# Another table of steps and engines for a three-layer kernel (attention, routed attention, convolution-gated FFN) on one core

## The chip, the core and the metric

The kernel runs on one NeuronCore of a Trainium2 chip. The metric is the device time of one execution in microseconds. Five engines work side by side, each through its own list of instructions in order: TensorE (PE, matmuls and transposes into PSUM banks), VectorE (DVE), ScalarE (ACT), GpSimd (POOL) and SyncE (SP), which here only issues DMAs. An engine stops at an instruction until the semaphores it waits for are there, and everything behind it on that engine stops too.

## The reference

Three layers follow each other, in float32. First, causal attention of 4 batches, 12 heads, 448 positions, 64 values a head. Second, a layer of four experts, each a small attention with its own weights, of which two are chosen for a position by a gate. Third, a feed-forward layer with a convolution of three taps over the positions and a sigmoid gate.

```python
attn_out = softmax(mask(q @ k.T / 8)) @ v                    # 4 x 12 heads, 448 x 448, causal
x = concat_heads(attn_out)                                   # 4 x 448 x 768
logits = x @ w_gate; w = softmax over the 2 largest of 4 experts
out = sum_e [e chosen] * w_e * softmax(mask(q_e @ k_e.T / 8)) @ v_e @ wo_e    # q_e, k_e, v_e = x @ wq/wk/wv[e]
h = relu(out @ w_in)                                         # 768 -> 1024
conv = conv_w[0]*h[s-1] + conv_w[1]*h[s] + conv_w[2]*h[s+1]
result = (h * sigmoid(conv)) @ w_out                         # 1024 -> 768
```

## The kernel before

Heads are worked in pairs: job A(b, p) is pair p (6 of them) of batch b in the first layer, job M(b, p) a pair of experts (2) in the second. The 448 positions are four blocks of 112. In a head, PE makes the scores of a block of rows (L632, L675), DVE their negative maximum over the causal part and a copy into SBUF (`rowmax`, L688, into P_A or P_M), ACT the exponential with its sum (`soft`, L697), DVE the reciprocal of the sums (L705, L708), one of three engines the scaling by it (`norm`, through `copy`, L349 on ACT, L351 on POOL, L355 on DVE), PE the transposes of the probabilities (L728), ACT or DVE their evacuation into PT (`evac`), and PE the product with v (L799).

For precision most operands of matmuls are split in two: hi, a rounded copy, and lo, the operand minus hi; a product is then three matmuls. So around the attention there is much work from SBUF to SBUF: `hi` is a `copy` (L349, L351, L355) and `lo` a subtraction (`two`, L358, on POOL or DVE). This is done for q and k of the later batches (nat into sk_A), for the weights of the experts (praw into wqk and wvg), for w_in (wraw over wm into whl, then folded with wo on PE at L920, three pieces of 12 matmuls a quarter), and for w_out (woraw over wom into wohl, with sums and differences of blocks, `combine`, for a multiplication scheme of 7 in place of 8 block products). The wohl tiles go to DRAM and come back as ws for the last stage, where PE multiplies them (L1473) with operands that are again split from SBUF tiles (ux, up, us, uq, uv).

All this is laid down as 3108 steps with what each needs and frees. A step's engine can be one of several:

```python
def of_two(n):
    return {"POOL": pool_tt(n), "DVE": dve(n)}
def of_one(n):
    return {"POOL": pool_ts(n), "DVE": 60 + 0.54 * n, "ACT": act_sb(n)}
```

Nothing is decided there when the kernel is built: a packed table, `ORDER`, lists all steps in one sequence, each with the engine it runs on, and `Program.run` (called at L1582) emits them in that order. So the table alone sets what stands before what in the list of each engine, which engine does a step, which PSUM bank a step gets, and when SP issues a DMA. `run` keeps a rough account of times only to put short runs of filler matmuls (L1580) where PE is likely to stand idle.

Of the kernel before, what the change touches and what calls it, by code (L numbers as in the profile page):

```python
# [1644 lines left out]
```

## Time and profile before

| | us |
|---|---|
| runs of the kernel | 489.45, 487.45, 489.25; median 489.25 |
| the profiled execution | 490.9 |
| its span, first to last instruction | 489.1 |

| engine | busy us | share of the span | instructions |
|---|---|---|---|
| PE | 476.2 | 97% | 3126 |
| DVE | 394.3 | 81% | 1145 |
| ACT | 342.9 | 70% | 956 |
| POOL | 346.4 | 71% | 491 |

The profile is of one execution. Busy time of PE includes time in which a matmul waits in its pipeline, so that the timeline's idle times before a matmul are what tells of a wait. In a timeline row a bracket at the end says how long the engine was idle before the first instruction of the row, and which instruction ended that. The mean granted clock of PE over the span is 0.991 of 2.4 GHz.

### The profile page before, as it was taken

The numbers are of one execution on the slowest core, as the hardware profiler recorded it, in microseconds if no ns is written. First come the engines' busy times: TensorE is split into PE (matmuls) and PEld (weight loads), VectorE is DVE, ScalarE is ACT, GpSimd is POOL, SyncE is SP. The second block draws the span as 40 slices with busy tenths as digits, with TensorE's granted clock in tenths as the row PEclk, the third lists the DMA queues.
The fourth block names the chain that finished last, engine by engine and source line by source line (L and its number), as shares of the span: only waits on it lengthen the run. The fifth ranks groups of instructions, "written<-read, shape, count | busy, mean of one in ns | idle before, by whom it ended". The sixth has DMA issues, their size and how long they took to land.

```text
span 489.1 us, 9977 instructions
## 1 busy us (share of the span) xinstructions
PE 476.2 (97%) x3126; PEld 401.3 (82%) x3126; DVE 394.3 (81%) x1145; ACT 342.9 (70%) x956; POOL 346.4 (71%) x491
## 2 busy tenths in 40 slices
PE   8999999999899999999999989999999999999996
PEld 7667787889679788878988867888789999999986
DVE  4899996999999888998789986277879987886372
ACT  3999987999888778998888976168985654432100
POOL 3969987879888768898888874015686486794820
PEclk9899999999999999999999989999999999999999
DMA  6854657988866964796874638364756676752022
GB/s 188 254 168 131 174 157 190 255 269 227 251 202 188 272 195 123 206 256 193 255 189 139 154 111 278 124 231 161 238 199 209 254 257 215 238 192 94 20 76 95
DMA packets 45413, 93.26 MB, mean 191 GB/s; under 512 B 4784, under 2 KB 26800, under 8 KB 45360
## 3 DMA queue, kind: packets, MB, share of 16 engines
q1 hardware_dynamic: 45360, 92.63, 63.3%
q8 instruction: 25, 0.41, 0.4%
q14 instruction: 28, 0.23, 0.2%
HBM read 60.72 MB, written 25.69 MB: 177 GB/s over the span
## 4 chain that ended last, share of the span: by engine, by line
PE 81%; ACT 6%; DVE 5%; POOL 3%; DMA 2%; issue 2%; POOLq 0%; DVEq 0%; ACTq 0%
PE bank L1473 21%; PE bank L799 11%; PE bank L993 11%; PE bank L728 10%; PE bank L675 9%; PE bank L1340 8%; PE bank L1044 6%; ACT P_A L697 3%; PE bank L632 3%; DMA woraw<-in_w_out_dram 2%; PE bank L920 2%; DVE P_A L688 2%; PE bank L1580 2%; POOL P_A L351 1%; ACT P_A L349 1%
## 5 line engine op out<-in xcount | busy, mean ns | idle before, releaser
L697 ACT ACTIVATE P_A<-P_A,nm_A 112x448 f32<-112x448 f32 (+3 forms) x192 | 99.6, 521 | 17.1 <-DVE nm_A L688 14.9
L688 DVE CUSTOM_DVE_ANT_0 P_A<-bank,mask 112x448 f32<-112x448 f32 (+3 forms) x192 | 78.6, 440 | 14.6 <-PE bank L632 7.9
L358 POOL TENSOR_TENSOR sk_A<-nat,sk_A 128x448 fp32r<-128x448 f32 (+1 forms) x70 | 81.2, 1160 | 8.2 <-ACT sk_A L349 2.6
L993 PE MATMUL bank<-xT,wqk 128*128 128x448 f32 x288 | 66.4, 372 | 0.0
L728 PE MATMUL bank<-ident,P_A 112*112 112x112 f32 x480 | 60.8, 265 | 2.5 <-ACT PT_A L349 1.4
L351 POOL TENSOR_SCALAR P_A<-P_A,r_A 112x224 f32<-112x224 f32 (+3 forms) x99 | 48.9, 507 | 12.2 <-PE bank L675 3.5
L728 PEld LDWEIGHTS bank<-ident,P_A 112*112 112x112 f32 x480 | 49.2, 135 | 9.6 <-ACT PT_A L349 2.4
L993 PEld LDWEIGHTS bank<-xT,wqk 128*128 128x128 f32 x288 | 51.8, 188 | 4.4 <-DVE lg L1064 0.5
L675 PE MATMUL bank<-sk_A 128*112 128x112 f32 (+3 forms) x288 | 51.8, 307 | 1.4 <-DVE nm_A L688 1.2
L799 PE MATMUL bank<-PT_A,v 112*64 112x448 f32 (+3 forms) x384 | 49.9, 405 | 0.2 <-DVE xT L831 0.2
L1473 PE MATMUL bank<-up,ws 128*128 128x448 f32 x198 | 48.5, 366 | 0.0
L1361 DVE SCALAR_TENSOR_TENSOR bank<-h,cw,bank 128x448 f32<-128x448 f32 x64 | 43.4, 686 | 5.2 <-ACT bank L1359 4.2
L799 PEld LDWEIGHTS bank<-PT_A,v 112*64 112x64 f32 x384 | 25.4, 136 | 23.5 <-issue 12.3
L675 PEld LDWEIGHTS bank<-sk_A 128*112 128x112 f32 x288 | 39.7, 175 | 5.9 <-DVE nm_A L688 1.5
L1044 PE MATMUL bank<-wvg,xT 128*112 128x260 f32 x288 | 44.2, 292 | 0.1
L349 ACT ACTIVATE P_A<-P_A,r_A 112x448 f32<-112x448 f32 (+3 forms) x83 | 41.4, 527 | 3.9 <-DVE r_A L708 3.8
L349 ACT ACTIVATE PT_A<-bank 112x336 f32<-112x336 f32 (+1 forms) x92 | 41.3, 469 | 2.9 <-PE bank L728 2.5
L351 POOL TENSOR_SCALAR P_M<-P_M,r_M,g_w 112x112 f32<-112x112 f32 (+3 forms) x61 | 35.6, 595 | 9.7 <-DVE r_M L708 5.5
L1473 PE MATMUL bank<-us,ws 128*128 128x448 f32 x171 | 41.4, 367 | 0.0
L1473 PEld LDWEIGHTS bank<-up,ws 128*128 128x128 f32 x198 | 37.2, 188 | 3.3
L1044 PEld LDWEIGHTS bank<-wvg,xT 128*112 128x112 f32 x288 | 36.8, 177 | 1.9 <-issue 1.5
L697 ACT ACTIVATION_READ_ACCUMULATOR P_A<-P_A,nm_A 112x1 f32 x192 | 36.8, 192 | 0.0
(184 smaller groups left out, 1069.1 us busy)
## 6 DMA issues: line engine op xcount, KB each, us to landing
nat<-in_qk_dram SPq DMA_DIRECT2D x72, 224.0 KB, 4.1
ws<-wset SPq DMA_DIRECT2D x7, 1536.0 KB, 7.7
wset<-wohl SPq DMA_DIRECT2D x18, 512.0 KB, 4.1
g<-g SPq DMA_DIRECT2D x32, 224.0 KB, 2.5
wraw<-in_w_in_dram SPq DMA_DIRECT2D x12, 512.0 KB, 5.2
woraw<-in_w_out_dram SPq DMA_DIRECT2D x12, 512.0 KB, 5.6
v<-in_v_dram SPq DMA_DIRECT2D x24, 224.0 KB, 5.0
out_dram<-osb_c SPq DMA_DIRECT2D x24, 224.0 KB, 2.0
```

What stands on the lines that cost most here:

```text
L349: nc.scalar.activation(dst, src, AF.Copy, scale=scale)
L351: nc.gpsimd.tensor_scalar(dst, src, scale, 1.0 if scale2 is None else scale2, ALU.mult, ALU.mult)
L358: (nc.gpsimd if e == "POOL" else nc.vector).tensor_tensor(dst, a, b, op)
L675: nc.tensor.matmul(sp[:CP], t[:, j.o[h], m * CP : (m + 1) * CP], t[:, j.o[h] + k, :w], start=(k == 2), stop=(k == 1),)
L688: nc.vector.tensor_tensor_reduce(rows(i), st["s", i][:CP, :w], mask[:, S - w :], -SCALE, 3.0e38, ALU.add, ALU.min, st["nm"][:, i : i + 1],)
L697: nc.scalar.activation(rows(i), rows(i), AF.Exp, bias=st["nm"][:, i : i + 1], scale=-1.0, accum_out=st["sm"][:, i, 0:1],)
L728: nc.tensor.transpose(pt[:CP, o : o + CP], rows(i)[:, kt * CP : (kt + 1) * CP], ident[:CP, :CP])
L799: nc.tensor.matmul(st["ov"][h * D : (h + 1) * D, kt * CP : S], j.v[:, kt, h, :], j.PT[h][:, col_base[kt] : col_base[kt] + S - kt * CP], st ...
L993: nc.tensor.matmul(st["ps"][:, :S], proj["wqk"][:, a, cc, w, p * P : (p + 1) * P], xT[b, cc][:, b2, :], start=(cc == 0 and (a, b2) == PASS ...
L1044: nc.tensor.matmul(st[i][:CP, :VW], xT[b, cc][:, a, i * CP : (i + 1) * CP], proj["wvg"][:, b2, cc, :], start=(cc == 0 and (a, b2) == PASSE ...
L1361: nc.vector.scalar_tensor_tensor(y, h, w, y, ALU.mult, ALU.add)
L1473: nc.tensor.matmul(ps(pb)[:, :S], wset[s][:, a, m, c2 * P : (c2 + 1) * P], unit(operands[q, c2, name][0])[:, b2], start=(c2 == 0 and (a, b ...
```

## The change

Only the table `ORDER` is another: the same 3108 steps, in another sequence, with another engine for 345 of them. It comes from a search over sequences and engines in which a DVE step from SBUF to SBUF that coincides with work on POOL was charged extra time; that charge isn't in the kernel's code. Its rows tell a reader nothing, so one of each side is shown.

```diff
--- before.py
+++ after.py
@@ -27,74 +27,74 @@
 
 ENGINES = ("ACT", "DVE", "PE", "POOL", "SP", "")
 ORDER = (
-    "c-jrt$4}b{gD_xMa0UNdz!hA<6<om;cW?z)+_6n&B_LS|NLB(ep9Ew+2}o7~@~%Y5N|dY=U=Bd$03?S%a-hrs$R0461CSgjIZ)n}D6`V{J%7c6"
...
+    "c-jrt$4}b{gD_xM+;In2a0OS~!4+J=75sAncMO@8fMg{gSqaE|5|H^MAXy2McO^<zqGY8&=0KSPkQ{*I0Avn8_JGM8C^-bk0m!=&kXh;bp1<P3"
...
 )
```

Counted in the built programs, PE has the same matmuls in both (2785 as listed, the same 23 filler instructions in runs of 10, 11 and 2), and SP the same 293 instructions. The counts that differ most:

| step | on DVE | on POOL | on ACT |
|---|---|---|---|
| two-input steps of the last stage (L358, ux, up, us, uq, uv) | 28 to 42 | 52 to 38 | |
| the same, both inputs in one tile | 9 to 5 | 7 to 11 | |
| hi of wohl, 512 columns | 10 to 13 | | 8 to 5 |
| hi of wohl, 256 columns | 2 to 4 | | 4 to 2 |
| lo of whl | 3 to 0 | 9 to 12 | |
| subtraction of halves of wom | 3 to 1 | 9 to 11 | |
| normalisation of P_A, 336 columns | 7 to 0 | 25 to 23 | 16 to 25 |
| hi of sk_A from nat | 1 to 1 | 21 to 18 | 14 to 17 |

All SBUF-to-SBUF steps of L353, L355 and L358 on DVE together are 5 more.

The first place is the hi step of wohl_1_4 of the last conversion of w_out (numbers 4017 before and 4087 now): the third score row maximum of a head follows it on DVE. DVE before (the rows that only fetch a maximum are left out in the lists of DVE):

```order
L688 ISA P_A_5_1_3997,nm_A_5_1_3998<-bank_62,mask 112x448
...
L355 TENSOR_SCALAR wohl_1_4_4017<-wom_1_1_3830 128x512
L688 ISA P_A_5_1_3997,nm_A_5_1_3998<-bank_65,mask 112x336
...
L688 ISA P_A_5_1_3997,nm_A_5_1_3998<-bank_61,mask 112x112
...
L355 TENSOR_SCALAR PT_A_3_1_1_4022<-bank_63 112x336
```

DVE now:

```order
L688 ISA P_A_5_1_3970,nm_A_5_1_3971<-bank_62,mask 112x336
...
L688 ISA P_M_1_1_4010,nm_M_1_1_4011<-bank_61,mask 112x336
...
L355 TENSOR_SCALAR wohl_1_4_4087<-wom_1_1_3887 128x512
L705 TENSOR_REDUCE r_A_5_1_3972<-sm_88 112x4
L355 TENSOR_SCALAR PT_A_3_1_0_4018<-bank_63 112x336
L708 RECIPROCAL r_A_5_1_3972<-r_A_5_1_3972 112x4
L688 ISA P_A_5_0_4105,nm_A_5_0_4106<-bank_61,mask 112x224
```

The hi step stands behind two row maxima as it did, but behind it comes the sum and reciprocal of P_A_5_1's rows (L705, L708), and the evacuation of PT; the next row maxima are those of another head.

POOL at the same place, before:

```order
L351 TENSOR_SCALAR P_A_3_1_3796<-P_A_3_1_3796,r_A_3_1_3798 112x112
L358 TENSOR_TENSOR wom_1_1_3830<-wom_1_0_3829,wom_1_1_3830 128x256
L351 TENSOR_SCALAR P_A_3_0_3868<-P_A_3_0_3868,r_A_3_0_3870 112x448
L358 TENSOR_TENSOR wohl_1_0_3993<-wom_1_0_3829,wohl_1_0_3993 128x512
L358 TENSOR_TENSOR sk_A_5_3885<-nat_5_0_3886,sk_A_5_3885 128x448
L358 TENSOR_TENSOR sk_A_5_3885<-nat_5_0_3886,sk_A_5_3885 64x448
L358 TENSOR_TENSOR wom_1_0_3829<-wom_1_1_3830,wom_1_0_3829 128x256
L358 TENSOR_TENSOR wom_1_0_3829<-wom_1_0_3829 128x256
L351 TENSOR_SCALAR P_A_5_1_3997<-P_A_5_1_3997,r_A_5_1_3999 112x448
L358 TENSOR_TENSOR wohl_1_4_4017<-wom_1_1_3830,wohl_1_4_4017 128x512
```

POOL now:

```order
L358 TENSOR_TENSOR wohl_1_0_4033<-wom_1_0_3886,wohl_1_0_4033 128x512
L358 TENSOR_TENSOR wom_1_1_3887<-wom_1_0_3886,wom_1_1_3887 128x256
L358 TENSOR_TENSOR wom_1_0_3886<-wom_1_1_3887,wom_1_0_3886 128x256
L358 TENSOR_TENSOR wom_1_0_3886<-wom_1_0_3886 128x256
L358 TENSOR_TENSOR wohl_1_4_4087<-wom_1_1_3887,wohl_1_4_4087 128x512
L351 TENSOR_SCALAR P_A_5_1_3970<-P_A_5_1_3970,r_A_5_1_3972 112x224
L351 TENSOR_SCALAR P_A_5_1_3970<-P_A_5_1_3970,r_A_5_1_3972 112x336
L351 TENSOR_SCALAR P_A_5_1_3970<-P_A_5_1_3970,r_A_5_1_3972 112x448
```

Before, the norm of P_A_3_0, the lo of wohl_1_0 and two lo steps of sk_A_5 stood there, ready without DVE's hi; now the lo steps of sk_A_5 stand further ahead, and behind the three wom steps come the lo of wohl_1_4 itself and the norms of P_A_5_1, which need the reciprocal that stands behind the hi step on DVE.

The second place is the difference of the halves of wom_1_1 in the second batch's conversion (1632 before, 1667 now). DVE before:

```order
L688 ISA P_A_5_1_1761,nm_A_5_1_1762<-bank_65,mask 112x448
...
L688 ISA P_A_5_1_1761,nm_A_5_1_1762<-bank_62,mask 112x112
...
L358 TENSOR_TENSOR wom_1_1_1632<-wom_1_1_1632 128x256
L708 RECIPROCAL r_A_4_0_1641<-r_A_4_0_1641 112x4
L355 TENSOR_SCALAR PT_M_0_1_0_1700<-bank_64 112x336
L688 ISA P_A_5_1_1761,nm_A_5_1_1762<-bank_61,mask 112x336
...
L355 TENSOR_SCALAR PT_M_0_1_0_1700<-bank_63 112x336
```

POOL now:

```order
L358 TENSOR_TENSOR wohl_1_6_1778<-wom_1_1_1667,wohl_1_6_1778 128x256
L351 TENSOR_SCALAR P_A_4_0_1633<-P_A_4_0_1633,r_A_4_0_1635 112x336
L358 TENSOR_TENSOR wom_1_1_1667<-wom_1_1_1667 128x256
L351 TENSOR_SCALAR P_A_4_0_1633<-P_A_4_0_1633,r_A_4_0_1635 112x448
L358 TENSOR_TENSOR wohl_1_0_1811<-wom_1_0_1666,wohl_1_0_1811 128x512
L358 TENSOR_TENSOR wom_1_1_1667<-wom_1_0_1666,wom_1_1_1667 128x256
L358 TENSOR_TENSOR wom_1_0_1666<-wom_1_1_1667,wom_1_0_1666 128x256
L358 TENSOR_TENSOR wom_1_0_1666<-wom_1_0_1666 128x256
```

The first L358 step of wom_1_1 has gone from DVE, where a reciprocal, an evacuation and a row maximum stood behind it, to POOL, between two norms of P_A_4_0.

The third place is the third piece of w_in's first quarter (whl_2; 1130 before, 1104 now), whose lo PE needs for its last 12 matmuls of the quarter. POOL before:

```order
L358 TENSOR_TENSOR sk_A_1_1065<-nat_1_0_1066,sk_A_1_1065 128x448
L358 TENSOR_TENSOR sk_A_1_1065<-nat_1_0_1066,sk_A_1_1065 64x448
L358 TENSOR_TENSOR whl_1_1017<-wm,whl_1_1017 128x512
L351 TENSOR_SCALAR P_A_0_1_908<-P_A_0_1_908,r_A_0_1_910 112x112
L351 TENSOR_SCALAR sk_A_3_1116<-nat_3_1_1117 128x2x448
L358 TENSOR_TENSOR whl_2_1130<-wm,whl_2_1130 128x512
L351 TENSOR_SCALAR P_A_1_1_982<-P_A_1_1_982,r_A_1_1_984 112x448
L351 TENSOR_SCALAR P_A_0_1_908<-P_A_0_1_908,r_A_0_1_910 112x224
```

POOL now:

```order
L351 TENSOR_SCALAR whl_1_1036<-wm 128x512
L358 TENSOR_TENSOR sk_A_1_1022<-nat_1_0_1023,sk_A_1_1022 64x448
L358 TENSOR_TENSOR whl_1_1036<-wm,whl_1_1036 128x512
L351 TENSOR_SCALAR whl_2_1104<-wm 128x512
L358 TENSOR_TENSOR whl_2_1104<-wm,whl_2_1104 128x512
L351 TENSOR_SCALAR P_A_1_1_970<-P_A_1_1_970,r_A_1_1_972 112x448
L351 TENSOR_SCALAR P_A_0_1_903<-P_A_0_1_903,r_A_0_1_905 112x448
```

The hi of sk_A_3 from nat_3_1 stood between the lo of whl_1 and the lo of whl_2. Now it isn't on POOL (it is on ACT), the hi of whl_2 has come from ACT, and whl_1's lo, whl_2's hi and its lo follow each other.

## Rows read from the trace of the kernel before

**Rows 1.** The page, part 1: busy us, share of the span, instructions.

```profile
PE 476.2 (97%) x3126; PEld 401.3 (82%) x3126; DVE 394.3 (81%) x1145; ACT 342.9 (70%) x956; POOL 346.4 (71%) x491
```

**Rows 2.** Stretches: us, busy us (instructions) by engine, PE clock, DMA share, GB/s.

```profile
280.00:300.00 20.00, 17.73 (x139) 14.85 (x137) 17.53 (x56) 15.98 (x51) 15.36 (x21) 0.91 0.58 179
420.00:440.00 20.00, 20.00 (x100) 18.43 (x99) 16.98 (x26) 7.43 (x14) 17.36 (x15) 1.00 0.63 217
```

**Rows 3.** Timeline of PE: start us, us, what, in brackets idle before, releaser.

```profile
81.49 0.74 PE L920 MATMUL bank<-whl,woT 128*128 128x256 f32 x4 [1.06 <-POOL whl L358]
...
125.95 0.43 PE L675 MATMUL bank<-sk_A 128*112 128x448 f32 x1 [0.70 <-DVE nm_A L688]
...
127.12 0.36 PE L675 MATMUL bank<-sk_A 128*112 128x224 f32 x1 [0.54 <-DVE nm_A L688]
...
168.32 0.59 PE L728 MATMUL bank<-ident,P_A 112*112 112x112 f32 x4 [0.95 <-ACT PT_A L349]
...
286.11 0.53 PE L675 MATMUL bank<-sk_M 128*112 128x224 f32 x1 [2.27 <-DVE nm_A L688]
```

**Rows 4.** Timeline of DVE, around 283 us.

```profile
282.57 3.06 DVE L355 TENSOR_SCALAR wohl<-wom 128x512 fp32r<-128x512 f32 x1
285.55 0.49 DVE L688 CUSTOM_DVE_ANT_0 P_A<-bank,mask 112x336 f32<-112x336 f32 x1
```

**Rows 5.** Timeline of POOL, around 283 us.

```profile
282.39 0.64 POOL L351 TENSOR_SCALAR P_A<-P_A,r_A 112x448 f32<-112x448 f32 x1
282.99 1.27 POOL L358 TENSOR_TENSOR wohl<-wom,wohl 128x512 fp32r<-128x512 f32 x1
284.23 2.40 POOL L358 TENSOR_TENSOR sk_A<-nat,sk_A 128x448 fp32r<-128x448 f32 x2
286.70 0.73 POOL L358 TENSOR_TENSOR wom<-wom,wom 128x256 f32<-128x256 f32 x1
```

**Rows 6.** Stretches behind the wait at 286 us, as in rows 2.

```profile
285.90:289.40 3.50, 3.29 (x14) 3.16 (x15) 2.56 (x14) 2.67 (x9) 2.19 (x3) 0.51 0.87 279
289.40:292.90 3.50, 3.50 (x30) 2.97 (x31) 3.37 (x19) 2.19 (x9) 2.08 (x3) 1.00 0.00 1
```

**Rows 7.** Groups by shape on DVE: xcount | busy us, mean ns | idle before.

```profile
L355 DVE TENSOR_SCALAR wohl<-wom 128x512 fp32r<-128x512 f32 x10 | 9.4, 942 | 0.0
...
L355 DVE TENSOR_SCALAR P_A<-P_A,r_A 112x336 f32<-112x336 f32 x7 | 4.4, 626 | 0.0
...
L358 DVE TENSOR_TENSOR wom<-wom 128x256 f32<-128x256 f32 x3 | 2.5, 829 | 1.0 <-POOL wohl L358 0.8 <-POOL wom L358 0.2
...
L358 DVE TENSOR_TENSOR wom<-wom,wom 128x256 f32<-128x256 f32 x2 | 0.8, 418 | 0.0
...
L355 DVE TENSOR_SCALAR whl<-wm 128x512 fp32r<-128x512 f32 x1 | 0.4, 427 | 0.0
```

**Rows 8.** Timeline of DVE, a normalisation of 336 columns.

```profile
298.55 0.39 DVE L355 TENSOR_SCALAR P_A<-P_A,r_A 112x336 f32<-112x336 f32 x1
```

**Rows 9.** Timeline of DVE, around 124 and 164 us.

```profile
123.43 1.47 DVE L358 TENSOR_TENSOR wom<-wom 128x256 f32<-128x256 f32 x1 [0.79 <-POOL wohl L358]
...
163.52 0.85 DVE L355 TENSOR_SCALAR P_A<-P_A,r_A 112x336 f32<-112x336 f32 x1
...
165.34 1.06 DVE L355 TENSOR_SCALAR wohl<-wom 128x512 fp32r<-128x512 f32 x1
```

**Rows 10.** Timeline of POOL, around 80 us.

```profile
79.26 0.95 POOL L351 TENSOR_SCALAR sk_A<-nat 128x896 fp32r<-128x896 f32 x1 [2.59 <-DMA nat<-in_qk_dram]
80.16 1.27 POOL L358 TENSOR_TENSOR whl<-wm,whl 128x512 fp32r<-128x512 f32 x1
```

**Rows 11.** Groups by shape on POOL, as in rows 7.

```profile
L351 POOL TENSOR_SCALAR whl<-wm 128x512 fp32r<-128x512 f32 x6 | 3.7, 622 | 1.8 <-DMA wset<-wohl 1.2 <-DVE r_A L705 0.5
```

**Rows 12.** Timeline of PE, 12 matmuls of one piece, around 273 us.

```profile
273.23 1.60 PE L920 MATMUL bank<-whl,woT 128*128 128x256 f32 x12
```

**Rows 13.** Waits of POOL: who waited for whom, total us, times, longest.

```profile
POOL sk_A L351 <- DMA nat<-in_qk_dram: 5.5, 3, 2.6
```

More of the change, by code (lines that the diff above doesn't have):

```diff
@@ L95 @@
[L95 to L97 removed]
+    "c-jrt$4}b{gD_xM+;In2a0OS~!4+J=75sAncMO@8fMg{gSqaE|5|H^MAXy2McO^<zqGY8&=0KSPkQ{*I0Avn8_JGM8C^-bk0m!=&kXh;bp1<P3"
+    "!gw$Vj0gwAX>cUG3)TaBf_sW<feqkZ;6`y%xHcFCriK||*RWd{0E@wFFgNT3_6-IDy@D^mm*G3`J@{+fTigI_81@D>2OEdIg!LA1;d%HmTnx9u"
+    "O>iGv17C-q!>{1O1?>e}@H;rDfCXEIZNb)H2e3SB8#Y?dUocTHU4SYe7SIbq@K$&?JPz-HcNVn6We5R6jQ|ia#C*Y0!FIt$ff3Py03-PYngVIT"
@@ new lines @@
+    "??_{Tw;)jf6xa%~1#Ji<(vBb^y@&zC5TXmwgWw`R7rZMtD!3@PFEE4Fkz2@X#4Un`6d_Lvte_lX0x^vMA@ay$WH0I*d4*IVS8!Ja!zcqXh>RiM"
+    "B32OZ5FXGVd>EdC?;<Bq2grHUA_|2fpze?$)E43Zaf&!ZoFnKcE@~U`8jeN~5p={Tsvk9tav*)kR%AD_2RVowMz$ffXgk`APT?Nl9^%$eo2YHn"
+    "G3q@AjA=o)p`|Dd%7k*Dyr=}K1C>Q}p?lCs5E4Vg0H`k17gPwHKz~MEpmOMO^Z@!E1wyMZXfzT1EBP7uJ?;bUIr$Id7;*>ql01Z-LC>Q<pg*Cx"
+    "m<i+z(us59!niBcE@l{ejyb^GVJ5JP=vDLq`V@VG7GY=@J;sLdU;s=K^APg@bA&m?ps;J$dF%o12)9K(BGa+wXjbtRhEpsp))eoMZ^$UhD3*X-"
+    "#NMLwXb_fz6=PLcA9fmhLf*jcVDHHLSR&{W+l?8-&_TTzE{K6Pqa&a(%mii_qsM+D|G=K&T8rC@$BO5R#h{7eAl8aaU^}pV#eLW=>>l|Tdx&kp"
@@ new lines @@
+    "4q!QG5QRW#E$k@lE__86qhp|ZEE>na5pV;=bjnaMm(p20M}A9QA@@<nC=(QOv7^{myg&hpTR;PpP0A8w7Bi1o!YC;q90&IiBf(8mtP~|^h_XuA"
+    "rtDMl6b4OA<I)z3r;FE$H;WB46Gck#QWBKDLN85;GvHci9h5H0BTy#@Ccp>=3r7kk3ISTKFiRl|m;$e$PXGumaJ`_MU;s1>8W8xYLFz5#taz`u"
+    "jTWR>X<v#z6<-wJ7q<%91v!w27Nd31dTCe1AlelLO(W25aQ8S+A*wJ*eLx+fZc+2p_vAl7tDsBD83jTmQE5~jRYWBf3ItMtMlc033FbgUv|}og"
+    "+E05)o1jipH$gj~N7PR0Q|dTvfx1LprS5}vsCm#C=o$4A#3<wyN($A5#zI@6rw}4k3ukG|w7)?hFbYfr4+&Oj<AN>PHjN?V3Ku|hutCTLOTilO"
+    "9`&5sDToPX1R~)z^(Pf21QpE-Rs<g5ciI(AO*K%xMSVrBML^LX&Q&Kt7!=-sjNn|+JZ;mt<4hGF(Dt2qr;Yka@IkODI1ro)h%Q2r6>Js8g#$(H"
@@ new lines @@
+    "MYDwqh0BHOg*Sp1)UCqZLJ#;S4Os-GtLd$DES*4Sx|sB@&KBV_;bWoH#ixIBUOVrcU{|E@P|#V#C>k%i6$}-jT=_zutDPPznkiDbdg*(GoFYll"
+    "Y2iiTd&VoUQy_4q3g?RqE~m>_WGiZSJ$Bs`-WPi50G)@I;8%*2MR}TmenM*#eiNwiJ;D(o1fLTc@pk+L{hIz4Lq?B)Cxu>o9KRskV0>cC2m$<("
+    "5RIqfAq*6wpT1gTr85{R#zs+$zFl-sbXwHo`pkIdx}|pzCJCMN!y*Es1^*DwWen5Li*oc%{8M}vfr!5;dWL_Fp9bF+0j?Rs5kBeS5yiwM!aP{d"
+    "5HUi;cH$D)#(0UJ!q4E};^*iq^cDOY`WwPH{g`pd=pjIgk;NXyL&h37PTT|&i`VcmaF)>mZU=wBuM%R67pzg%3)e5MAB-v19BW;8iVre2gzNNO"
+    "x{|m@KcWv3h6y|P&-e>`7q}Pv419w(5+O_!^BxZ&Y=b|8M+ql%8*xXtL3b0o8Aw78qm#&Ba+xCLCgC}Fhj2;wLikKjGd;{8)4&{Lj4>t{L;{1b"
@@ L98 @@
+    "^(EDv?n}Q-LX*FS9Vt)hB>p{)N{*zB8FJE=@F(cWu{1g}nVwC*iu{@CPj4o<No8_B38W?yGl}05=c#<skep8+rBBnOj6HLazDc*FtVvJuE)C0^"
+    "C9jgZ>Amz=W-_y$*~)k`9hvUTdGb01PIsnyQ$SLjj3--?pcE#>$b>TS%r6;UMx4=R2x)p6-F%u+Hz!m5snHZBZET*+EM%54eVM_`aE8>pn@Kbu"
+    "WS*z)k`t+&<VEH#)t=<0rRlL|M)OU^-h7|Yq)lmXb8B-)b9ZxZ^KZ@VDPoGA@;39DcbgBIkD5=L^BJJ|y!oHakCSt$`P9?oVrsH^wt1mh+`QEM"
+    "zWJ_Moi%2y>2P{2wUyn?9%SR`qwGocd)Ak>XT90YW+0o&j%6pav)P4gYqlfXo$brsWbd<(7IX_Fi_Vg=!_7<C_t}B$i!8B))xyYfv$E{}15+qE"
+    "(*"
 )
```

112 lines of the change are left out of this document (45 added, 67 removed).

## The prediction

> **What bounds the kernel now.** I read the page's busy times first: TensorE (PE) is busy 476.2 of the 489.1 us span [rows 1]. Then the stretches: from 300 us on PE never stops, 20.00 of 20.00 us busy from 420 to 440 us, although VectorE (DVE) and GpSimd (POOL) are also busy there 17.0 and 17.4 us; the one poor stretch is 280 to 300 us, with PE 17.73 us busy at a mean granted clock of 0.91 [rows 2]. The change gives PE the same matmuls, so its time can only move by what PE waits, and by the clock it is granted. I therefore went through PE's waits in the timeline and took those above half a microsecond after the start-up, five of them: 1.06 us at 81.5, 0.70 at 126.0, 0.54 at 127.1, 0.95 at 168.3 and 2.27 at 286.1 us [rows 3]. The reader is to see in the next views that four of the five lead back to one thing: a DVE step between two SBUF tiles that took far longer than its work because POOL was working.
>
> The largest shows it best. At 282.57 us DVE starts a copy of 512 columns, the hi part of a converted weight, and it takes 3.06 us; the row maximum for which PE waits is queued behind it and starts at 285.55 [rows 4]. On POOL three steps ran back to back in that time, 0.64, 1.27 and the first of a pair of 2.40 us [rows 5]. PE resumes at 286.11, and in the 3.50 us from 285.9 its granted clock is 0.51 and it does 14 matmuls; in the next 3.50 us, at full clock, it does 30 [rows 6]. So an idle PE is followed by a stretch at 1.2 in place of 2.4 GHz, and the wait is paid twice.
>
> **What the changed order removes.** The profiled execution took 490.9 us (span 489.1 and 1.8 around it); the median of the runs shown is 489.25, so I sum against 490.9 and scale by 489.25/490.9 = 0.9966.
>
> - At 286 us: 2.27 us of waiting [rows 3] and the slow stretch, 3.29 us busy at 0.51 of the clock, (1 - 0.51) x 3.29 = 1.6 us [rows 6]. Sum 3.9. In the new order the same hi step (wohl_1_4 of the last batch) has on POOL, behind the four steps that are ready earlier, only its own lo and norms of P_A_5_1, and both wait for something that DVE does at or after this step. Nothing can overtake it. POOL's four steps are 1.27 and three of 0.73, 3.46 us [rows 5]; DVE has eight steps between the hi of the piece before and this one, at 0.49 us [rows 4] about 3.9 us, an estimate. So POOL is empty when DVE arrives, and the copy should take its free time of 0.43 [rows 7]. I take the whole 3.9.
> - At 126 us: the DVE subtraction of two halves of wom, 256 columns, took 1.47 us [rows 9], against 0.42 for the same shape where nothing meets it [rows 7]. PE's two waits behind it sum to 1.24 [rows 3]; I take the 1.05 that the step lost. In the new order this subtraction is on POOL. The row maximum behind it no longer waits for it; the price of the POOL step is 0.73 [rows 5], on an engine for which PE doesn't wait there.
> - At 168 us: a normalisation of 336 columns on DVE took 0.85 against 0.39 [rows 8, 9], and a hi copy 1.06 against 0.43 [rows 7, 9]. Together 1.09 us late, and PE waits 0.95 through ACT's evacuation [rows 3]. The new order has no normalisation of 336 columns on DVE any more (7 before). I take 0.95.
> - At 81 us the cause is another: POOL stood 2.59 us waiting for a DMA (nat) to land before a hi copy of 0.95 us, with the lo step for which PE waited queued behind it [rows 10]. In the new order that hi copy is on ACT, and POOL's hi and lo of this piece (whl_2) follow its whl_1 steps directly. I take PE's 1.06 [rows 3].
>
> Removed: 3.9 + 1.05 + 0.95 + 1.06 = 7.0 us.
>
> **What it adds.** First, meetings elsewhere. DVE keeps about as many SBUF-to-SBUF steps (by the counts in the section on the change, 5 more). Up to 300 us the groups that lost most are the 512-column copies, 10 x (942 - 427) ns = 5.2 us, the wom subtractions, 3 x (829 - 418) = 1.2, and the 336-column normalisations, 7 x (626 - 390) = 1.7 [rows 7, 8]: 8.1 us in all, of which 2.27 + 1.05 + 0.95 = 4.3, or 53%, reached PE. The new order is clear at the places I followed, but it has 13 of the 512-column copies in place of 10, and I can't follow all. Bounds: 0, if all are placed like the ones above, and the same 4.3 with one slow clock of 1.6, if they meet POOL as before. I take half of the waiting and no slow clock, 2.1 us. Second, the two pieces at 81 us now follow each other on PE, 12 matmuls each, while POOL does hi 0.62 and lo 1.27 of the second [rows 10, 11]. The 12 matmuls of the first last 1.60 [rows 12], so PE waits between 0 (it comes late) and 1.89 - 1.60 = 0.3 us beyond the lo of the first; I take 0.3. Third, the engines' loads: 14 more two-input subtractions and additions of the last stage go to DVE and leave POOL. They lie beside a PE that is busy 20.00 of 20.00 us [rows 2]: 0. If that cover went, the price would be that of a DVE wait in the tail, a few tenths.
>
> Sum: 490.9 - 7.0 + 2.1 + 0.3 = 486.3 us for a profiled execution, times 0.9966 = 484.7 us.
>
> One rule of the Trainium skill speaks against the first term. In the trace the 512-column copy was held through the end of two POOL steps and most of a third [rows 4, 5]. The page "SBUF — State Buffer", section "Who interferes with whom", says that whichever of the two issues first holds the shared ports for that whole instruction and the other blocks, which I read as a wait of one instruction. By the rule the copy would have ended 0.43 us after POOL's first step, near 283.5 us, and PE's wait there would have another cause; by the row it ended at 285.6. The measurement decides the sum; the rule stands below as a rival.
>
> **The rivals.**
> - *The meetings only move.* For: about 100 DVE steps between SBUF tiles remain and POOL is busy 15 to 17 us in every 20 [rows 2]. Against: the places followed. Added back 4.3 + 1.6 in place of 2.1: 490.9 - 7.0 + 5.9 + 0.3 = 490.1, scaled 488.4.
> - *The lock lasts one instruction.* Then the wait at 286 us stays: 490.9 - 7.0 + 3.9 + 2.1 + 0.3 = 490.2, scaled 488.5. Against it stand the two POOL steps that both ran inside the copy.
> - *All meetings are gone.* No 2.1: 484.2, scaled 482.6.
> - *ACT takes over the wait for the DMA, and the kernel is slower.* ACT now makes 17 of the hi copies from nat in place of 14, and the one of 81 us is among them. POOL's waits for nat were 5.5 us in three, the longest 2.6 [rows 13], and only 1.06 of it reached PE, since POOL is seldom the engine PE waits for. On ACT the exponentials and evacuations that PE needs are queued behind the copy. Three waits of 2.6 that reach PE in full and one slow clock are 7.8 + 1.6 = 9.4: 486.3 + 9.4 = 495.7, scaled 494.0. It decides from 4.6 us (back to 490.9) and is measurably slower from 7.1 us. Against: on SP this load stands ahead of the woraw loads, as before, and the second of those no longer right behind the first.
>
> **How the numbers follow.** Forecast 0.40; all meetings gone 0.10; meetings move 0.26; lock of one instruction 0.05; ACT's wait, or another new wait of that size, 0.19. Within 0.5% (2.4 us, about what a measurement of this kernel can tell from no change) means 486.8 to 491.7. The forecast by itself covers 482.6 to 486.8 and counts as faster, as does the case above it: 0.50. The two that give 488.4 and 488.5 are no change: 0.31. The last is slower: 0.19. For 8 in 10 I go from 481.0, a little under the case without meetings, to 491.5, which leaves out most of the slower case (0.13 to 0.15) and little below.
>
> **What would show it.** Right: no DVE step between SBUF tiles above 1.5 us; the hi copy wohl_1_4 near 0.43 us; PE at full clock from 280 to 300 us and busy above 19 of 20; PE's named waits between 20 and 300 us down by some 5 us. Wrong in the first term: a second slow stretch of the clock elsewhere, behind a DVE copy of 1 us or more, or behind an ACT that waits for nat. If PE's waits fall and the time stays, the matmuls themselves have become slower, which I have no row for.

## The result, and the profile after

| kernel | runs | median us | from | to |
|---|---|---|---|---|
| before | 4 | 489.05 | 487.45 | 489.45 |
| after | 4 | 484.40 | 484.16 | 485.37 |

The ratio of the two is 0.9915, with an interval of 0.9889 to 0.9941: the kernel became 4.2 us faster (2.9 to 5.4). The profiled execution took 485.37 us, its span is 483.6.

The page's part 1 of the kernel after answers to [rows 1]:

```profile
PE 473.2 (98%) x3126; PEld 401.1 (83%) x3126; DVE 393.0 (81%) x1152; ACT 347.3 (72%) x965; POOL 332.9 (69%) x475
```

The span is shorter by 5.5 us, PE's busy time by 3.0 and its idle time (span less busy) by 2.5, from 12.9 to 10.4. The stretches of the kernel after, with the columns of [rows 2]:

```profile
120.00:140.00 20.00, 17.79 (x132) 13.58 (x131) 19.15 (x53) 16.06 (x45) 15.98 (x20) 0.91 0.74 216
280.00:300.00 20.00, 18.93 (x158) 15.12 (x159) 14.04 (x50) 14.34 (x47) 17.82 (x27) 1.00 0.49 155
420.00:440.00 20.00, 20.00 (x99) 18.37 (x98) 13.97 (x27) 5.34 (x10) 8.80 (x9) 1.00 0.63 207
130.20:133.70 3.50, 3.28 (x14) 2.93 (x15) 3.47 (x12) 3.50 (x10) 2.23 (x4) 0.52 0.80 240
133.70:137.20 3.50, 3.50 (x29) 2.35 (x28) 3.37 (x14) 2.89 (x10) 2.45 (x3) 1.00 0.98 283
285.90:289.40 3.50, 3.50 (x29) 1.85 (x29) 3.31 (x15) 3.50 (x14) 3.42 (x6) 1.00 0.62 193
```

The poor stretch has moved. From 285.9 us PE is at full clock and does 29 matmuls where it did 14 [rows 6]; from 130.2 us there is a new stretch at 0.52 with 14 matmuls. What ended PE's waits in the kernel after, with the total, the number and the longest:

```profile
PE bank L675 <- DVE nm_M L688: 2.2, 1, 2.2
PE bank L1580 <- POOL ident masks.py:199: 1.4, 1, 1.4
PE bank L728 <- POOL P_A L351: 1.0, 3, 0.5
PE bank L728 <- POOL P_M L351: 0.7, 1, 0.7
PE bank L728 <- ACT PT_A L349: 0.7, 2, 0.5
```

All five waits of [rows 3] are gone. In their place stand one of 2.2 us on DVE and four on POOL's normalisations, 1.8 in all, which lie at 279 to 294 us. ACT waits nowhere for the landing of nat. Three steps of DVE's timeline after answer to [rows 4] and [rows 7]:

```profile
126.08 3.05 DVE L355 TENSOR_SCALAR wohl<-wom 128x512 fp32r<-128x512 f32 x1 [0.22 <-POOL wom L358]
...
129.77 0.38 DVE L688 CUSTOM_DVE_ANT_0 P_M<-bank,mask 112x224 f32<-112x224 f32 x1
...
285.19 0.43 DVE L355 TENSOR_SCALAR wohl<-wom 128x512 fp32r<-128x512 f32 x1
```

The hi copy wohl_1_4 takes its free 0.43 us at 285.19. But another hi copy, of the second batch's conversion, takes 3.05 us at 126.08: the picture of [rows 4], at another place. POOL's timeline after, at both places:

```profile
126.02 0.64 POOL L351 TENSOR_SCALAR P_A<-P_A,r_A 112x448 f32<-112x448 f32 x1
126.63 2.22 POOL L358 TENSOR_TENSOR sk_A<-nat,sk_A 128x448 fp32r<-128x448 f32 x2
131.29 0.36 POOL L351 TENSOR_SCALAR P_A<-P_A,r_A 112x112 f32<-112x112 f32 x1 [2.44 <-DVE r_A L708]
...
284.41 1.79 POOL L358 TENSOR_TENSOR wom<-wom,wom 128x256 f32<-128x256 f32 x2
```

At 126 us POOL began 0.05 us ahead of DVE, with a normalisation and two lo steps of sk_A back to back, and the copy lasted to their end. At 285 us POOL was not empty either. The first step of the pair on wom makes the copy's input; by the single instructions in the trace the copy starts 0.03 us after that step has ended and 0.04 us ahead of the second. The second step took 0.97 us in place of 0.73 [rows 5], and DVE lost nothing. PE's timeline after, behind the first:

```profile
130.42 0.90 PE L675 MATMUL bank<-sk_M 128*112 128x336 f32 x2 [2.21 <-DVE nm_M L688]
```

### The profile page after: what moved, and what is told of

Its sections match the earlier page's. It is cut to its first block, busy times and chain, and to the rows that moved or that the text cites. A ratio compares the mean times of both kernels' runs of the same rounds, so it can differ in the third digit from the quotient of the medians.

```text
span 483.6 us, 9980 instructions
## 1 busy us (share of the span) xinstructions
PE 473.2 (98%) x3126; PEld 401.1 (83%) x3126; DVE 393.0 (81%) x1152; ACT 347.3 (72%) x965; POOL 332.9 (69%) x475
## 4 chain that ended last, share of the span: by engine, by line
PE 86%; DVE 5%; POOL 5%; ACT 3%; issue 1%; POOLq 0%; DVEq 0%; ACTq 0%
PE bank L1473 21%; PE bank L993 11%; PE bank L799 11%; PE bank L728 11%; PE bank L675 10%; PE bank L1340 8%; PE bank L1044 7%; PE bank L920 3%; PE bank L632 2%; DVE P_A L688 2%; PE bank L1580 2%; ACT P_A L697 2%; POOL P_M L351 1%; POOL P_A L351 1%; DVE wohl L355 1%
## 5 line engine op out<-in xcount | busy, mean ns | idle before, releaser
L697 ACT ACTIVATE P_A<-P_A,nm_A 112x224 f32<-112x224 f32 (+3 forms) x192 | 99.8, 524 | 11.7 <-DVE nm_A L688 11.2
L688 DVE CUSTOM_DVE_ANT_0 P_A<-bank,mask 112x448 f32<-112x448 f32 (+3 forms) x192 | 79.6, 440 | 12.3 <-PE bank L632 7.7
L358 POOL TENSOR_TENSOR sk_A<-nat,sk_A 64x448 fp32r<-64x448 f32 (+1 forms) x67 | 77.8, 1163 | 4.6 <-ACT sk_A L349 0.6
L351 POOL TENSOR_SCALAR P_A<-P_A,r_A 112x112 f32<-112x112 f32 (+3 forms) x95 | 48.3, 520 | 12.2 <-DVE r_A L708 10.4
L675 PE MATMUL bank<-sk_A 128*112 128x224 f32 (+3 forms) x288 | 51.9, 305 | 0.2 <-DVE nm_A L688 0.2
L349 ACT ACTIVATE P_A<-P_A,r_A 112x224 f32<-112x224 f32 (+3 forms) x94 | 46.5, 525 | 2.8 <-DVE r_A L708 1.6
L1473 PE MATMUL bank<-up,ws 128*128 128x448 f32 x198 | 46.7, 367 | 0.0
L1473 PE MATMUL bank<-us,ws 128*128 128x448 f32 x180 | 44.3, 366 | 0.0
L351 POOL TENSOR_SCALAR P_M<-P_M,r_M,g_w 112x336 f32<-112x336 f32 (+3 forms) x63 | 35.9, 585 | 2.9 <-ACT PT_A L349 1.4
```

Source lines behind the costliest of these rows:

```text
L349: nc.scalar.activation(dst, src, AF.Copy, scale=scale)
L351: nc.gpsimd.tensor_scalar(dst, src, scale, 1.0 if scale2 is None else scale2, ALU.mult, ALU.mult)
L358: (nc.gpsimd if e == "POOL" else nc.vector).tensor_tensor(dst, a, b, op)
L675: nc.tensor.matmul(sp[:CP], t[:, j.o[h], m * CP : (m + 1) * CP], t[:, j.o[h] + k, :w], start=(k == 2), stop=(k == 1),)
L688: nc.vector.tensor_tensor_reduce(rows(i), st["s", i][:CP, :w], mask[:, S - w :], -SCALE, 3.0e38, ALU.add, ALU.min, st["nm"][:, i : i + 1],)
L697: nc.scalar.activation(rows(i), rows(i), AF.Exp, bias=st["nm"][:, i : i + 1], scale=-1.0, accum_out=st["sm"][:, i, 0:1],)
```

## The experiments

Two measures recur. The ratio is to the kernel before on the same chip, with its 95% interval in brackets. PE's lead is read by lining up PE's matmuls by work done (each counted with the mean duration of its shape at full clock): how much earlier than in the profiled kernel before the same work is reached. Where two orders give PE its matmuls in another sequence it is good to some half a microsecond.

| PE's lead in us, where the kernel before is at (us) | 78 | 101 | 128 | 133 | 138 | 165 | 187 | 280 | 294 | 336 | 469 |
|---|---|---|---|---|---|---|---|---|---|---|---|
| after | 0.8 | 3.0 | 4.9 | 1.7 | 1.2 | 0.8 | 2.4 | 3.5 | 6.0 | 4.8 | 4.9 |
| b_286_act | 1.7 | 1.5 | 1.6 | 1.6 | 1.6 | 1.6 | 1.6 | 1.6 | 5.4 | 5.3 | 5.3 |
| b_four | 0.5 | 2.1 | 3.2 | 2.3 | 2.2 | 2.2 | 2.8 | 3.1 | 6.9 | 6.9 | 6.9 |
| a_three | 1.6 | 3.8 | 5.6 | 5.1 | 5.3 | 3.4 | 5.0 | 6.0 | 9.3 | 7.9 | 7.9 |

For b_286_act and b_four the first column is no effect of their edits, which lie behind it: the profiled kernel before has a stretch at clock 0.57 from 16 to 20 us, and these two have none. The new order has it in one of its two profiles (0.57 in after_again, 1.00 in after), the kernels made from the old order in one of four. With that stretch after_again still leads by 0.7 us at 78 us, so the 0.8 of after is not the clock's alone. At 128 us the new wait of the kernel after is still to come; at 138 us it and the slow stretch behind it are past.

**The 286 us place alone.** b_286_act: the kernel before with one step, the hi copy wohl_1_4, on ACT.

```diff
-    prog.run(steps_of(ORDER), warm)
+    at = {2358: "ACT"}
+    prog.run([(n, at.get(n, e)) for n, e in steps_of(ORDER)], warm)
```

> The kernel before with one step on another engine: the 512-column hi copy wohl_1_4 of the last conversion (3.06 us at 282.57 us) runs on ACT. Theory (POOL holds the copy, and PE's wait of 2.27 us and the half-clock stretch of 3.3 us hang on it): 2.3 to 3.9 us less than the kernel before, PE's longest wait after the start-up at 1.1 us, the clock full from 280 to 300 us. Rival (the lock is one instruction long and the wait there has another cause): within 0.5 us of the kernel before. Second rival (ACT, busy with exponentials, delays PE as much): 0 to 1 us less, with a new wait for ACT near 286 us.

Measured: 486.04 us (12 runs, 484.27 to 488.82) against 489.79, ratio 0.9941 [0.9915, 0.9967], 3.75 us less by the medians (1.6 to 4.2 by the interval); PE's lead grows by 3.7 us at that place and nowhere else. The stretch of [rows 6] in it:

```profile
285.90:289.40 3.50, 3.50 (x28) 2.77 (x28) 3.13 (x14) 3.50 (x15) 3.50 (x5) 1.00 0.43 158
```

28 matmuls at full clock in place of 14. By PE's lead the one copy that met POOL cost 3.7 us, the wait and the slow stretch together.

**The clock's share of it.** b_286_fill: the kernel before, with 10 filler instructions for PE in the wait at 286 us; DVE and POOL as before.

```diff
             if e == "PE":
+                if n == 1638:
+                    fill(10, None)
...
-        r = prog.idle_bank(since)
+        r = 6 if since is None else prog.idle_bank(since)
```

> The kernel before with 10 filler matmuls (some 0.21 us each, into a PSUM bank that is free) on PE ahead of the scores that wait 2.27 us at 286.1 us; nothing else is changed, and the copy on DVE stays held. Theory (idle PE is followed by a stretch at half clock, the second part of the prediction's 3.9 us): clock 1.00 from 285.9 to 289.4 us in place of 0.51, and 1.2 to 1.8 us less than the kernel before. Rival (the clock falls for another reason): clock 0.5 there as before, within 0.4 us. Second rival (the fillers run past the wait): 0 to 0.5 us more.

Measured: 488.98 us (12 runs) against 490.32, ratio 0.9975 [0.9958, 0.9991], 1.34 us less (0.4 to 2.1). Its stretch, and PE's timeline (the fillers are L1582, the score matmuls L677, two lines further down here):

```profile
285.90:289.40 3.50, 3.43 (x28) 2.91 (x27) 3.47 (x21) 2.92 (x11) 2.22 (x3) 1.00 0.87 278
```

```profile
283.65 2.39 PE L1582 MATMUL bank<-ident 128*128 128x128 f32 x20
286.11 0.62 PE L677 MATMUL bank<-sk_M 128*112 128x224 f32 x4
```

PE resumes at 286.11 as it did [rows 3], and the stretch behind is at full clock. PE's lead grows by 1.3 us at this place. So the 3.75 us split into some 2.4 of waiting and 1.3 of a slow clock, which an idle PE had brought on.

**The 81 us place alone.** b_81_act: the kernel before with the hi copy for which POOL waited [rows 10] on ACT (`at = {798: "ACT"}`, in the form above).

> The kernel before with one step on another engine: the hi copy from nat that waits 2.59 us for its DMA on POOL at 79.3 us runs on ACT, at the same place in the sequence. Theory of the prediction (it only frees POOL): PE's wait of 1.06 us at 81.5 us goes, 0.7 to 1.4 us less than the kernel before. Rival (ACT takes over the wait for the DMA, and PE's needs are queued behind it): a wait of ACT for that DMA of 2 us or more, PE waits 1 to 2.6 us near 80 us, and the kernel takes 0 to 2 us more.

Measured: 489.86 us (12 runs) against 490.32, ratio 0.9995 [0.9974, 1.0017]. ACT's, POOL's and PE's timelines:

```profile
78.38 0.95 ACT L349 ACTIVATE sk_A<-nat 128x896 fp32r<-128x896 f32 x1 [2.71 <-DMA nat<-in_qk_dram]
79.24 0.61 ACT L349 ACTIVATE whl<-wm 128x512 fp32r<-128x512 f32 x1
...
79.94 1.27 POOL L358 TENSOR_TENSOR whl<-wm,whl 128x512 fp32r<-128x512 f32 x1 [4.21 <-ACT whl L349]
...
81.27 1.58 PE L920 MATMUL bank<-whl,woT 128*128 128x256 f32 x11 [0.97 <-POOL whl L358]
```

The wait went to ACT, whl_2's hi step was queued behind it there, POOL's lo behind that, and PE still waited 0.97 us. To change the engine is not enough; what helped in the new order is that whl_2's hi and lo stand ahead of the step that waits for the DMA, as the next kernel bears out at this place.

**Four places by hand.** b_four: the kernel before with 2358 on ACT, the subtraction 2241 of 126 us on POOL, the normalisation 1256 of 164 us on ACT, the hi copy 2330 a little later on DVE, and 798 behind the lo of whl_2 on POOL; all else in the old order.

```diff
+    at = {2358: "ACT", 2241: "POOL", 1256: "ACT"}
+    steps = [(n, at.get(n, e)) for n, e in steps_of(ORDER) if n not in (798, 2330)]
+    for n, e, behind in ((798, "POOL", 38), (2330, "DVE", 1241)):
+        steps.insert(1 + [k for k, _ in steps].index(behind), (n, e))
```

> The kernel before with the four places of the prediction mended by hand and nothing else of the new order: the hi copy at 282.6 us on ACT, the difference of wom at 123.4 us on POOL, the normalisation at 163.5 us on ACT and the hi copy at 165.3 us behind the evacuation that PE waits for, and the hi copy from nat at 79.3 us behind the lo of whl_2 on POOL. Theory (the prediction's removed terms, 7.0 us, sit at these places): 5.5 to 7.5 us less than the kernel before, which is below the new order. Rival (the gain of the new order is spread over many small waits, and what is taken away here comes back behind it): 2 to 4.5 us less.

Measured: 484.71 us (6 runs) against 489.79, ratio 0.9909 [0.9880, 0.9938], the new order's gain within the intervals. The 5.1 us by the medians lie between the two expectations, and the interval (3.0 to 5.9) reaches into both. The largest groups of PE's waits that are left behind the start-up:

```profile
PE bank L728 <- ACT PT_A L349: 1.3, 4, 0.6
PE bank L675 <- DVE nm_A L688: 0.8, 2, 0.6
```

Five moved steps of 3108 do as much as the whole new table. What else the table moves sums to about nothing by these times; among it are the new waits at 130 us and at 279 to 294 us.

**The new meeting at 126 us.** a_126_behind: the kernel after with that hi copy, its lo and its store behind the row maximum for which PE waited (2251, 2252, 2253 behind 575).

> The new order with one copy moved: the hi of wohl_1_2 that starts at 126.08 us and takes 3.05 us (its lo and its DMA with it) stands behind the three row maxima that PE waits for. Theory (this meeting costs the new order PE's wait of 2.21 us and, where the clock falls behind it, up to 1.7 more): 2.0 to 3.9 us less than the new order, so about 480.5 to 482.4 where that takes 484.4; PE has no wait above 1 us after 20 us. Rival (the row maxima are late for another reason, or the wait moves to what stands behind the copy): within 0.7 us of the new order.

Measured: 484.43 us (6 runs), ratio 0.9904 [0.9876, 0.9932], the same as after. DVE's and PE's timelines:

```profile
126.79 2.31 DVE L355 TENSOR_SCALAR wohl<-wom 128x512 fp32r<-128x512 f32 x1
...
131.06 0.85 PE L728 MATMUL bank<-ident,P_A 112*112 112x112 f32 x7 [2.40 <-ACT PT_A L349]
```

The copy came 0.71 us later and ended at 129.10 us in place of 129.13, both times 0.28 us after POOL's row of steps; PE's wait only moved, from a row maximum on DVE to an evacuation on ACT, 2.40 us in place of 2.21. So the copy's end is set by POOL's row, and another order of DVE's steps around it was no cure.

a_126_lo: the kernel after with the two sk_A lo steps (1212, 1216) later on POOL, behind a normalisation.

> The new order with two POOL steps moved: the two lo steps of sk_A (2.22 us back to back) that run while the copy at 126.08 us is held stand behind the next normalisation, which POOL can start only after DVE's reciprocal. Theory (POOL's row holds the copy): the copy takes 0.43 to 1.1 us, PE's wait of 2.21 us there falls below 0.5, and the kernel takes 1.5 to 2.5 us less than the new order, 481.9 to 482.9 where that takes 484.4. Rival (another thing holds the copy): it still takes about 3 us, no change. Second rival (as with the copy moved: the wait comes back behind it, here through the lo steps that are late): copy short, time within 0.7 us of the new order.

Measured: 482.61 us (5 runs), ratio 0.9862 [0.9840, 0.9884], 1.8 us better than after (its slowest run took 483.69 us, the fastest of after 484.16). DVE's, POOL's and PE's timelines:

```profile
125.91 0.43 DVE L355 TENSOR_SCALAR wohl<-wom 128x512 fp32r<-128x512 f32 x1 [0.22 <-POOL wom L358]
...
129.54 2.12 DVE L355 TENSOR_SCALAR wohl<-wom 128x512 fp32r<-128x512 f32 x1
...
125.85 0.91 POOL L351 TENSOR_SCALAR P_A<-P_A,r_A 112x448 f32<-112x448 f32 x1
...
129.12 3.55 POOL L358 TENSOR_TENSOR sk_A<-nat,sk_A 128x448 fp32r<-128x448 f32 x3
...
134.76 0.86 PE L728 MATMUL bank<-ident,P_A 112*112 112x112 f32 x7 [1.18 <-DVE PT_A L355]
```

The copy is free, and POOL's normalisation pays (0.91 in place of 0.64). The moved steps hold another copy for 2.12 us, and PE waits 1.18 later on. A meeting moved once more, to a cheaper place.

**What holds a copy.** Three kernels that only do DVE and POOL steps tell how long a DVE step is held. In the first, each row of POOL steps begins with a normalisation of 128 rows:

> This kernel leaves the whole computation out and writes zeros: it times single DVE steps while POOL works through a row of steps, in one-core trials that start with an empty POOL. DVE first evacuates PSUM (0.6 us), then does one step between SBUF tiles: a copy of 512 columns or a two-input step of 512 columns. Held until the row pauses (my theory): the copy alone takes about 0.43 us, beside one-input step and one two-input step about 0.43 + what is left of both (near 1.7), and about 1.27 more for each further two-input step (near 4.2 with three, 6.8 with five); a two-input DVE step (0.69 alone) the same way. One instruction (rival, the Trainium skill's page SBUF - State Buffer, section Who interferes with whom): no copy above 0.43 + 1.27 = 1.7 us, whatever stands behind. Several and then a turn (second rival, after the copy of 282.6 us, which ended before the fourth step did): the copy's time grows up to two or three steps and stays there, near 3.1 us. A step that reads PSUM stays at 0.6 in all three.

Measured: alone the copy takes 0.42 us; beside POOL 0.58 to 0.59 whatever the row's length, here eight steps (DVE's and POOL's timelines):

```profile
29.59 5.10 POOL L65 TENSOR_SCALAR t<-t,t 128x448 f32<-128x448 f32 x8 [0.31 <-DVE t L74]
29.92 0.59 DVE L56 TENSOR_SCALAR t<-t 128x512 fp32r<-128x512 f32 x1
```

It is let in when POOL's first step ends. That is one step and no row, and not what the kernel's copies showed, so the theory of a whole row fell for these rows. In the second, the rows begin with 112 rows, as the kernel's normalisations do, and the copy's start is varied:

> This kernel leaves the whole computation out and writes zeros. As in the trials before it DVE does one step between SBUF tiles beside a row of POOL steps, but the moment at which DVE's step starts is swept in ten stages over POOL's first and second step, and the rows begin with a one-input step of 112 rows or with a two-input step. In the trials before it no copy took more than 0.59 us, one boundary of POOL's steps, while the copies at 282.6 us (kernel before) and 126.1 us (new order) were held through two or three. Theory A (the moment decides): in the same row some starts give 0.6 us and others 1.7 us or more. Theory B (the kind of step decides): a copy that starts in a two-input step is passed over by the next two-input step, so 1.7 to 4.2 us in the row of three of them for every start, and 0.6 where it starts in the one-input step. Theory C (POOL's row alone never holds it): no copy above 0.43 + 1.27 = 1.7 us in any row.

Measured: both engines' timeline, for two starts:

```profile
15.20 0.90 POOL L58 TENSOR_SCALAR t<-t,t 112x448 f32<-112x448 f32 x1 [0.31 <-DVE t L68]
15.26 0.42 DVE L49 TENSOR_SCALAR t<-t 128x512 fp32r<-128x512 f32 x1
...
18.85 0.64 POOL L58 TENSOR_SCALAR t<-t,t 112x448 f32<-112x448 f32 x1 [0.31 <-DVE t L68]
18.98 3.24 DVE L49 TENSOR_SCALAR t<-t 128x512 fp32r<-128x512 f32 x1
19.45 2.48 POOL L61 TENSOR_TENSOR t<-t,t 128x512 fp32r<-128x512 f32 x2
```

A copy that starts 0.06 us behind POOL's step is free and POOL pays (0.90 for 0.64); one that starts 0.13 us behind it lasts to the row's end, 3.24 us, and so did every later one, up to 0.87 us behind. The moment decides only whether the copy is held at all, and the expectation that no copy takes above 1.7 us fell. This is the kernel's picture at 126 us, where the copy was held from 0.05 us behind on. For that at 286 us one trial has POOL's row of [rows 5], a normalisation and three two-input steps:

```profile
122.76 0.64 POOL L58 TENSOR_SCALAR t<-t,t 112x448 f32<-112x448 f32 x1 [0.31 <-DVE t L68]
122.93 3.06 DVE L49 TENSOR_SCALAR t<-t 128x512 fp32r<-128x512 f32 x1
123.36 3.61 POOL L61 TENSOR_TENSOR t<-t,t 128x512 fp32r<-128x512 f32 x3
```

The copy takes 3.06 us, as in the kernel [rows 4]. By the single instructions POOL stands still for 0.08 us ahead of its fourth step, in the trial and in the kernel, and the copy gets in there: it was held through three whole steps, and not through "two POOL steps and most of a third", as the prediction read it. The third varies the rows:

> This kernel leaves the whole computation out and writes zeros. Trials as before, each row of POOL steps at four starting moments of DVE's step, all of them moments at which POOL already works. In the first trials a copy that started in a one-input step of 128 rows got its turn at that step's end (0.59 us); in the second, one that started in a step of 112 rows was held to the end of the row (3.2 us). Theory P (the number of rows of POOL's step): rows that begin with a step of 128 rows give 0.5 to 1.1 us, those with 112 or 64 rows 1.5 to 3.4, and three steps of 112 rows 1.5 or more against 0.6 for three of 128. Theory D (the operands' number of rows, DVE's against POOL's): the same, but turned round for a copy of 112 rows. Theory Q (what differs is how full POOL's queue is, not the step): all rows with two or more steps behind give 1.5 us or more here, those of 128 rows too.

Measured, by the copy's start behind that of POOL's row (S, s: one input, 128 and 112 rows; t: two inputs):

| row | +0.13 | +0.33 | +0.59 | +0.86 |
|---|---|---|---|---|
| S t t | 0.79 | 0.59 | 0.42 | 1.29 |
| s t t | 3.24 | 3.03 | 2.77 | 2.50 |
| s s s | 0.78 | 0.58 | 0.42 | 0.67 |
| s S t | 0.83 | 0.64 | 0.42 | 1.90 |

The last column of the first two rows, in both engines' timeline:

```profile
15.23 0.64 POOL L66 TENSOR_SCALAR t<-t,t 128x448 f32<-128x448 f32 x1 [0.31 <-DVE t L73]
15.83 2.66 POOL L63 TENSOR_TENSOR t<-t,t 128x512 fp32r<-128x512 f32 x2
16.08 1.29 DVE L53 TENSOR_SCALAR t<-t 128x512 fp32r<-128x512 f32 x1
...
29.45 0.64 POOL L66 TENSOR_SCALAR t<-t,t 112x448 f32<-112x448 f32 x1 [0.47 <-DVE t L73]
30.05 2.48 POOL L63 TENSOR_TENSOR t<-t,t 128x512 fp32r<-128x512 f32 x2
30.32 2.50 DVE L53 TENSOR_SCALAR t<-t 128x512 fp32r<-128x512 f32 x1
```

Both copies start in the first two-input step. The one ends with that step, the other with the row, and the rows differ only in whether the step ahead had 128 or 112 rows. Rows of one-input steps let the copy in at the next step even with 112 rows, which the expectation had wrong. In s S t a copy that starts in the S is held to the row's end (1.90) although that step has 128 rows, so it is not the step just ahead alone. A first step of 64 rows does as one of 112 (3.23 at +0.13), and a copy of 112 rows fares as one of 128 (0.78 and 3.24 in the first two rows), so it is no mismatch of rows between the two engines. A two-input DVE step is held too: 0.68 us free, 1.04 in S t t and 3.50 in s t t at +0.13. Why the chip does so is open: no run here looks inside.

**A better order.** after_again is the kernel after once more; a_three is it with the edit of a_126_lo, a second hi copy with its lo and store (2246, 2247, 2248) behind the evacuation that PE needs, and one normalisation of the 280s (1878) on ACT.

> The new order once more, on the chip of this call, to have it beside the next kernel: 484.0 to 485.0 us, 0.988 to 0.993 of the kernel before. Its half-clock stretch behind the wait at 130 us is there in some executions only (mean clock 0.996 and 485.4 us in the one, 0.999 and 484.2 us in others).

> The new order with three edits: the two lo steps of sk_A at 126.6 us behind the next normalisation, as in the run before (482.6 us); the hi copy at 129.5 us of that run, which was held 2.12 us beside them, behind the four steps that decode the next piece of w_in; and one normalisation of P_A at 276 us (336 columns), for which PE waited 0.55 and 0.23 us on POOL, on ACT, which is idle there for 1.85 us. Theory (both waits go): 0.8 to 1.9 us less than the run before it, 480.7 to 481.8. Rival (DVE is short of time behind 129 us in any case, so the wait of 1.18 us at 134.8 us only moves): 0.3 to 0.8 us less, by the normalisation alone. Second rival (PE's waits at 277 us end on another normalisation): no gain, 482.3 to 483.

Measured on one chip: after_again 484.22 us (4 runs), ratio 0.9873 [0.9850, 0.9896]; a_three 482.32 (5 runs), ratio 0.9824 [0.9806, 0.9842], faster than both kernels. POOL's, DVE's and PE's timelines of after_again at 126 us:

```profile
126.24 0.91 POOL L351 TENSOR_SCALAR P_A<-P_A,r_A 112x448 f32<-112x448 f32 x1
...
126.30 0.43 DVE L355 TENSOR_SCALAR wohl<-wom 128x512 fp32r<-128x512 f32 x1 [0.21 <-POOL wom L358]
126.76 3.12 DVE L358 TENSOR_TENSOR wohl<-wom,wohl 128x512 fp32r<-128x512 f32 x1
...
130.44 0.56 PE L675 MATMUL bank<-sk_M 128*112 128x336 f32 x2 [2.00 <-DVE nm_M L688]
```

In this execution the copy, 0.06 us behind POOL's normalisation, was free and POOL paid, and the lo step behind the copy was held 3.12 us: nearly the same price at the same place, 2.00 us for PE, by another victim. In a_three PE has two waits above half a microsecond between 60 and 300 us, in PE's timeline:

```profile
136.06 1.57 PE L920 MATMUL bank<-whl,woT 128*128 128x256 f32 x11 [0.97 <-POOL whl L358]
...
288.67 1.01 PE L728 MATMUL bank<-ident,P_M 112*112 112x112 f32 x7 [0.80 <-POOL P_M L351]
```

The first is new. POOL does the same steps there as in a_126_lo, half a microsecond earlier; PE, which no longer waits the 1.18 us ahead of it, comes to this lo of whl sooner and waits. So that wait mostly moved, as the first rival had it. The second was 0.74 in the kernel after; the one of 0.54 us on P_A ahead of it is gone. Beside a_126_lo, on another chip, the further two edits show 0.3 us by the medians, the least that this rival gave, which the intervals don't tell from nothing.

## Why the prediction was right, point by point

The time (484.7 predicted, 484.4 measured), the sign and the mechanism held: PE gained by the loss of waits behind DVE steps that met POOL, and of the slow clock behind the largest. The parts held unevenly.

- *The 3.9 us at 286 us.* Right, and shown alone: 3.75 by b_286_act, of which 1.34 is the clock by b_286_fill (1.6 predicted). The reason given was not right: "POOL is empty when DVE arrives". POOL was at work. The copy was free because it started between two of POOL's steps, 0.03 us after the one that makes its input, and POOL paid 0.24. It is so in all five profiles of kernels with the new order (0.42 or 0.43 us).
- *The 1.05, 0.95 and 1.06 us.* The waits of [rows 3] are gone in the kernel after. By PE's lead, b_four gains 1.6 us around 81 us, 0.2 from there to 133 us and 0.6 at 168: the first was worth more than its term, the other two less in that kernel, since PE there still waits 0.65 and 0.61 us for what comes next. The reason named for 81 us, that the hi copy is on ACT, is by b_81_act worth nothing; the other one named, that whl_1's lo and whl_2's hi and lo follow each other, is what counts.
- *The 2.1 us of new meetings.* Too small in the profiled execution, and wrong in kind. The step was "half of the waiting and no slow clock". The runs show one meeting for which PE waits, 2.21 and 2.00 us in the two profiles, and a slow stretch behind it in both (0.52 in 3.50 us from 130.2 us; 0.57 in 4.00 us from 132.0): (1 - 0.52) x 3.28 = 1.6 us in the profiled one, 3.8 with the wait, and PE's lead falls by 3.7 from 128 to 138 us. Four of the eight runs of after and after_again have a mean clock of 0.999 or 1.000, and so no such stretch, which takes some 0.003 off it (0.996 in the profiled run of after); in those runs the term is nearer to its 2.1. "No DVE step between SBUF tiles above 1.5 us" failed at 3.05, and "a second slow stretch of the clock elsewhere", named as what would speak against the first term, came without the first term being wrong.
- *Nothing for POOL's new steps.* Wrong by 1.8 us: the normalisations that stand behind the wom and lo steps on POOL come late at 279 to 294 us, and PE's lead falls there from 6.0 to 4.8. I followed what can overtake the hi copy, not who waits for POOL behind it.
- *What offset these.* By PE's lead the 5.5 us of the two profiles are 0.8 before 78 us, 2.2 at 81, 1.9 up to 128, -3.7 up to 138, -0.4 up to 165, 1.6 at 168, 1.1 up to 280, 2.5 at 286, -1.2 behind it, 0.1 after 336 us, and 0.6 in the last stage. The 2.2, 1.9 and 1.6 are 2.6 more than their three terms, and of the 1.9 the two waits that are gone make 1.24. For the 0.8, the -0.4, the 1.1 and the 0.6 I have no row that explains them, and they stay open. The forecast for the profile was 4.6 (490.9 to 486.3). Gains that came out larger than their terms nearly cancel the added waits, which did so too: that the sum came within a microsecond is in part luck.
- *PE's named waits between 20 and 300 us* fell from 6.4 to 4.8 us, by 1.6 and not by 5, for the two reasons above; from 280 to 300 us PE was 18.93 and not above 19 busy, for the second.
- *The rivals.* That ACT takes over the wait for nat is refuted in the kernel after, and shown at small scale by b_81_act. That the meetings only move was half right: it is what happened at 126 us, with a wait and a slow clock as this rival had them (3.8 us where it priced 5.9), but it left the gain of 286 us. The lock of one instruction is refuted for the kernel's rows. The Trainium skill, "SBUF — State Buffer", "Who interferes with whom", has whoever issues first hold the shared pair for the whole instruction: the 0.59 us of the first kernel on ports agree, the 3.24 us through three instructions don't, and the measurement decides.
